# Hash attention with two MLP layers on one core: the products with the values of a pair of heads in one stretch of TensorE's queue, behind the projections for the next pair's hash bits

## The chip, the cores and the metric

The kernel runs on one core of one Trainium2 chip. The metric is the device time of one execution in microseconds (us). TensorE (PE in the profile) does all matrix products, VectorE (DVE) and ScalarE (ACT) read the products out of PSUM and do the elementwise work, GpSimd (POOL) does a little of it, and SyncE (SP) issues the DMAs.

## What is computed

The reference, cut to what matters here (scale is 1/8, B, H, S, D = 2, 8, 768, 64; n_bits is 6):

```python
q_bits = (np.einsum('bhsd,dk->bhsk', q, proj) > 0)      # the same for k
q_bucket = np.sum(q_bits * 2 ** np.arange(n_bits), axis=-1)
mask = q_bucket[:, :, :, None] == k_bucket[:, :, None, :]
scores = np.where(mask, scale * np.matmul(q, k.transpose(0, 1, 3, 2)), -1e9)
attn = np.exp(scores - np.max(scores, axis=-1, keepdims=True))
attn = attn / (np.sum(attn, axis=-1, keepdims=True) + 1e-09)
x = np.matmul(attn, v)                                  # heads joined: 1536 x 512
h = np.maximum(x @ w_in, 0.0)                           # first MLP, 512 -> 2048 -> 512
x = h * h @ w_out
h = x @ moe2_w_in                                       # second MLP, the same sizes
out = (np.maximum(h, 0.0) + alpha * np.minimum(h, 0.0)) @ moe2_w_out
```

A query attends only to the keys that have the same six sign bits. Everything is computed in float32, for the MLPs and the scores as sums of rounded high and low parts.

## The kernel before, in words

The 1536 tokens are four chunks of 384 (`T`). A chunk's attention is four pairs of heads; a pair lies with one head on partitions 0 to 63 and the other on 64 to 127. The attention of chunk 0 runs alone (`attention_first`). Then the first MLP of chunk c (`feed_forward`, lines 811 on) runs with the attention of chunk c + 1 woven into it (`attention_beside`): `attention_beside` returns a list of steps, and the object `following` calls the next of them at the slots of the MLP's loops. The last part, the second MLP (from line 1161 on), has no attention beside it. The change is in `attention_beside` alone, so in the twelve pairs of chunks 1 to 3.

For one such pair the work on TensorE is this. **The projections** (line 254 in `hash_bits`): the keys (`kr`, 768 columns, for an even chunk only, that is for the pairs of chunk 2, since chunk 3 uses the keys of chunk 2 again) and the queries (`qn`, 384 columns) are multiplied with `proj_sb`. The array is used as four strips of 32 columns, one for each quarter of the tokens, so that one product writes 32 partitions of the bank; VectorE makes bits of it (line 258). **The matches** (line 276): the bits with `code`, on the whole array. **The scores** (line 426): four products for each of the six blocks u of 128 queries (three blocks t for each head h), on the whole array; VectorE takes the maximum (`low`, line 434), ScalarE the exponential and its sum (`sm`, line 435). **The transposes** (line 451): six of `sm` per block, three to a bank `m`, copied to `pt` by ScalarE (456) or VectorE (458). **The products with the values** (line 472 in `blocks`): `vr`, six blocks of 128 keys, with `pt`. One head's product uses the left 64 columns of the array, the other's the right 64, twelve products in all, summed in one bank `o`, which ScalarE then copies to `u` (478). The profile has two instructions for each float32 product, so the twelve count as 24. **The reciprocal** (`recip`): a small transpose (486) of the sums, a copy `rrow` (488), a DMA to DRAM (498) and two back (`rb`, 501). `finish` multiplies `u` with `rb` and splits the result in `xh` and `xl` (517 to 519), which the next chunk's MLP reads.

The MLP's products beside it are lines 750 to 752 (hidden layer) and 791, 792, 795 (back to 512 columns), all on the whole array. While the two run side by side, the banks `m` are two, for the projections, the matches, the transposes, `o` and the reciprocal in turn; the scores have one pair of banks.

Each engine runs its own queue in the order in which the instructions stand there. The order is made when the kernel is built: steps in program order, and within that by priorities (`tc.high_priority`), so that an instruction of high priority is put ahead of others that are ready. Before the change, the three parts of the products with the values of a pair are three steps (`values(old, 0)`, then two more), woven between the MLP's products like every other step; the projections are made at the start of a pair's preparation (`first` for the keys, `q_split` for the queries). A pair's preparation runs during the pair ahead of it.

Of the kernel before, what the change touches and what calls it, by code (L numbers as in the profile page):

```python
# [9 lines left out]
BF16 = mybir.dt.bfloat16  # L10
U32 = mybir.dt.uint32
AX = mybir.AxisListType
AF = mybir.ActivationFunctionType
ALU = mybir.AluOpType
# [13 lines left out]
URGENT = 100  # L28
# [3 lines left out]
def kernel(  # L32
# [20 lines left out]
    nc = tc.nc  # L53
    B, H, D, S = qT.shape
    NB = N_BITS
    NT, DM = out.shape
    P = 128
# [154 lines left out]
    class Pair:  # L212
# [5 lines left out]
        def __init__(self, c, j):  # L218
            self.c, self.j = c, j
            self.b = c // 2  # L220
            self.first = c == 0 and j == 0
            self.awaited = c == 0 and j == NPAIR - 1
            self.p = {}
            self.pt = {}

        def pe(self, ins):

# [20 lines left out]
        def hash_bits(self, x, n):  # L248

            w = n // NG  # L250
            bits = p1.tile([P, S // NG], BF16, tag="bits", name="bits")[:, 0:w]
            ps = m_tile()
            for g in range(NG):
                self.pe(nc.tensor.matmul(
                    ps[g * GR:(g + 1) * GR, 0:w], proj_sb.rearrange("p h n -> p (h n)"), x[:, g * w:(g + 1) * w],
                    start=True, stop=True,
                ))
            self.next(nc.vector.tensor_scalar(bits, ps[:, 0:w], 0.0, None, ALU.is_gt))
            return bits

        def matches(self, bits, n):

# [33 lines left out]
                nc.sync.dma_start(out=f32(self.k[r, h]), in_=f32(kh[r]).unsqueeze(1).to_broadcast([D, 2, S]))  # L296

        def k_ids(self):
            y = self.matches(self.bits, S)
            ids = self.kr[:, 0].bitcast(F32R).rearrange("p (a n) -> p a n", n=T)  # L300
            for x, to in [(y[a], ids[:, a]) for a in range(2)] if self.c == 0 else [(y, ids)]:
                nc.vector.tensor_scalar(to, x, pop, -1.0, ALU.not_equal, ALU.mult)  # L302
            for h in range(2):
                r, o = self.rows(h)
                ins = nc.sync.dma_start(out=f32(self.k[o, h]), in_=self.kr[r])
            keyed[self.c, self.j] = ins

            tc.keep_in_program_order(load_values(self.b, self.j))
            self.vr = keys[self.b, self.j][-1]

        def q_split(self):
            self.new_q()
            self.bits = self.hash_bits(self.qn, T)
            if self.c == 0:
                for h in range(2):
                    self.q_halves(h)
                return
            self.q3 = state["q3"].tile([P, 3, T], F32R, tag="q3", name="q3")
            qh = self.q3[:, 1]
            nc.scalar.activation(qh, self.qn, AF.Copy, scale=scale)  # L320
            nc.vector.scalar_tensor_tensor(self.q3[:, 2], self.qn, scale, f32(qh), ALU.mult, ALU.subtract)
            for h in range(2):
                r, o = self.rows(h)
                nc.sync.dma_start(out=f32(self.q[r, h]), in_=f32(self.q3[r, 1:3]))
# [9 lines left out]
            ))  # L334

        def q_ids(self):
            y = self.matches(self.bits, T)
            if self.c == 0:
                self.q_yes(y)
                return  # L340
            nc.scalar.activation(self.q3[:, 0], y[:, 0, :], AF.Relu, bias=off, scale=FAR)
            for h in range(2):
                r, o = self.rows(h)
                nc.sync.dma_start(out=f32(self.q[o, h]), in_=f32(self.q3[r, 0:2]))
# [54 lines left out]
        def prepare(self):  # L399

            def ahead():
                c, j = divmod(self.c * NPAIR + self.j + 1, NPAIR)
                if c < NCH:
                    load_pair(c, j)

            def first():
                ahead()
                self.start()
                if self.c % 2 == 0:
                    self.k_bits()  # L410
                else:
                    self.q_split()

            if self.first:
                return [self.at_once, ahead]
            if self.c % 2:
                return [first, self.q_ids]
            return [first, self.k_split, self.k_ids, self.q_split, self.q_ids]
# [23 lines left out]
        def p_t(self, h, t, a):  # L442
            if t == 0 and a == 0:
                by = "third" if self.c == 0 and (2 * self.j + h) % 3 == 2 else "p2"
                self.pt[h] = state[by].tile([P, NTB, NKB, P], F32, tag="pt", name="pt")
            pp = self.p[h, t]
            ps = m_tile()
            n = NKB // 2
            for i in range(n):
                b = a * n + i  # L450
                self.pe(nc.tensor.transpose(ps[:, i * P:(i + 1) * P], pp[:, b * P:(b + 1) * P], ident))  # L451
            src = ps[:, 0:n * P].rearrange("p (b n) -> p b n", b=n)
            dst = self.pt[h][:, t, a * n:(a + 1) * n, :]
            with self.urgent():
                if EVICT[self.c][2 * t + a] == "a":
                    nc.scalar.activation(dst, src, AF.Copy)
                else:
                    nc.vector.tensor_copy(dst, src)  # L458

        def av(self, part):  # L460

            n = NKB // 3
            self.blocks(part * n, (part + 1) * n)

        def blocks(self, b0, b1, t0=0, t1=NTB):

# [104 lines left out]
    def attention_beside():  # L571
# [9 lines left out]
        def turn(pr, u):  # L581
            for a in range(2):
                steps.append(lambda a=a: pr.p_t(*divmod(u, NTB), a))

        def values(pr, part):
            steps.append(lambda: pr.av(part))

        def finish(pr):
            steps.append(pr.finish)
# [1 line left out]
                ends.append(len(steps))  # L591

        steps += [begin] + pairs[0].prepare()
        last = 2 * NTB - 1
        for n, pr in enumerate(pairs):
            old = pairs[n - 1] if n else None
            prep = pairs[n + 1].prepare() if n + 1 < len(pairs) else []
            for u in range(2 * NTB):
                steps.append(lambda pr=pr, u=u: pr.scores(*divmod(u, NTB)))
                if prep and u != 1:  # L600
                    steps.append(prep.pop(0))
                if u == 0 and old:
                    turn(old, last)
                    steps.append(old.recip)
                    values(old, 0)
                if u == 1 and old:
                    values(old, 1)
                    values(old, 2)
                if u:
                    turn(pr, u - 1)  # L610
                if u == 4 and prep:
                    steps.append(prep.pop(0))
                if u == (3 if old and old.j == NPAIR - 1 else last) and old:
                    finish(old)
            assert not prep
        turn(pr, last)
        steps.append(pr.recip)
        for part in range(3):
            values(pr, part)
        finish(pr)  # L620
        return steps, ends

# [635 lines left out]
```

## Time and profile before

| what | value |
|---|---|
| median of three runs | 787.2 us (785.86 to 789.8) |
| the profiled execution's own time | 787.25 us |
| its span from the first instruction to the last | 785.5 us |
| PE busy | 764.5 us, 97% of the span |
| DVE busy | 543.0 us, 69% |
| ACT busy | 509.8 us, 65% |
| POOL busy | 143.0 us, 18% |
| granted TensorE clock, mean | 0.997 of full speed |

The profile is of one execution. Its own time is 1.75 us longer than its span. An engine counts as busy while one of its instructions runs; waiting, branching and issuing DMAs don't count. Matmuls overlap each other, and their ends are modelled, so that the step from one start to the next is the better measure of what a product costs.

### The profile page before, as it was taken

Reading aid. Unit: us, or ns where it says so; the run is one execution under the profiler, and the core shown is the slowest. Engines: PE = TensorE matmul, PEld = TensorE weight load, DVE = VectorE, ACT = ScalarE, POOL = GpSimd, SP = SyncE. Lnnn points to the kernel's source line nnn. Section 1 sums busy time; section 2 is a strip of 40 time slices with the busy share of each in tenths; the row PEclk is TensorE's granted clock in tenths of the full one; section 3 lists DMA queues with packets and bytes.
Section 4 is the critical chain, followed back from the end, with each engine's and each line's share of the span. In section 5 each row is a group of like instructions: output and inputs, shape, how many; then the busy total and the mean of one; then the engine's idle time right before and its main releaser. Section 6 shows DMA issues by size and latency. Waiting matters only on the chain.

```text
span 785.5 us, 12375 instructions
## 1 busy us (share of the span) xinstructions
PE 764.5 (97%) x4354; PEld 633.0 (81%) x4354; DVE 543.0 (69%) x957; ACT 509.8 (65%) x990; POOL 143.0 (18%) x88
## 2 busy tenths in 40 slices
PE   6889999999999999999999999999999999999998
PEld 4556777877878777787787889999998889999886
DVE  7668789888778777997887856745665914666111
ACT  7769788777756646766675667856776534777331
POOL 1000000000000000000000001004657534657440
PEclk9999999999999999999999999999999999999999
DMA  5865888887878786887767685351311236321222
GB/s 164 216 191 188 250 279 266 273 231 224 227 237 255 213 237 219 304 256 268 243 214 238 202 281 203 113 163 60 129 41 55 67 109 224 130 75 51 58 67 93
DMA packets 56705, 143.65 MB, mean 183 GB/s; under 512 B 7402, under 2 KB 11652, under 8 KB 56644
## 3 DMA queue, kind: packets, MB, share of 16 engines
q1 hardware_dynamic: 56644, 142.87, 58.5%
q8 instruction: 34, 0.56, 0.3%
q14 instruction: 27, 0.22, 0.1%
HBM read 96.62 MB, written 25.47 MB: 155 GB/s over the span
## 4 chain that ended last, share of the span: by engine, by line
PE 62%; DVE 2%; DMA 2%; issue 0%; ACT 0%; SPq 0%; ACTq 0%
PE b L1081 6%; PE b L1080 6%; PE b L1086 5%; PE b L948 5%; PE b L947 5%; PE b L946 5%; PE m L472 3%; PE s L426 3%; PE h L750 3%; PE m L451 3%; PE h L752 2%; PE h L751 2%; PE acc L791 2%; PE acc L795 2%; PE acc L792 2%; PE acc L774 1%
## 5 line engine op out<-in xcount | busy, mean ns | idle before, releaser
L983 POOL TENSOR_TENSOR wp<-wraw,wp 128x1024 fp32r<-128x1024 f32 (+1 forms) x32 | 68.2, 2135 | 501.4 <-ACT wp L980 488.6
L712 ACT ACTIVATE wh<-wf 128x512 fp32r<-128x512 f32 x128 | 79.7, 629 | 55.2 <-PE h L751 24.4
L713 DVE TENSOR_TENSOR wl<-wf,wh 128x512 fp32r<-128x512 f32 x128 | 88.6, 699 | 32.9 <-ACT wh L712 32.6
L435 ACT ACTIVATE sm<-s,low 128x768 f32<-128x768 f32 x84 | 75.4, 898 | 35.7 <-DVE low L434 35.1
L434 DVE TENSOR_REDUCE low<-s 128x1 f32<-128x768 f32 x84 | 80.2, 955 | 14.6 <-PE s L426 13.1
L451 PE MATMUL m<-ident,sm 128*128 128x128 f32 x525 | 84.1, 276 | 4.7 <-DVE kr L302 1.6
L451 PEld LDWEIGHTS m<-ident,sm 128*128 128x128 f32 x525 | 64.1, 140 | 25.8 <-issue 2.7
L750 PE MATMUL h<-xh,wh 128*128 128x384 f32 x212 | 77.8, 367 | 1.2 <-ACT r L757 0.9
L426 PE MATMUL s<-k,q 128*128 128x384 f32 x336 | 77.7, 352 | 0.0
L1080 PE MATMUL b<-wp,gp 128*128 128x512 f32 x192 | 75.1, 391 | 0.0
L948 PE MATMUL b<-xph,wp 128*128 128x384 f32 x224 | 74.9, 334 | 0.0
L946 PE MATMUL b<-xph,wp 128*128 128x384 f32 x224 | 74.9, 334 | 0.0
L947 PE MATMUL b<-xpl,wp 128*128 128x384 f32 x224 | 74.9, 334 | 0.0
L1081 PE MATMUL b<-wp,gp 128*128 128x512 f32 x192 | 74.8, 390 | 0.0
L752 PE MATMUL h<-xh,wl 128*128 128x384 f32 x212 | 72.3, 341 | 0.0
L1070 POOL TENSOR_TENSOR gp<-g,gp 128x768 fp32r<-128x768 f32 x32 | 62.2, 1949 | 51.4 <-ACT gp L1067 50.7
L751 PE MATMUL h<-xl,wh 128*128 128x384 f32 x212 | 71.5, 337 | 0.0
L1064 DVE TENSOR_TENSOR wp<-wp 128x512 fp32r<-128x512 f32 x28 | 26.3, 950 | 61.7 <-ACT wp L1061 57.8
L426 PEld LDWEIGHTS s<-k,q 128*128 128x128 f32 x336 | 58.0, 190 | 10.5 <-ACT sm L435 3.7
L458 DVE COPY pt<-m 128x384 f32<-128x384 f32 x96 | 53.1, 553 | 18.5 <-PE m L451 17.9
L791 PE MATMUL acc<-wh,gh 128*128 128x512 f32 x144 | 64.6, 448 | 0.0
L792 PE MATMUL acc<-wl,gh 128*128 128x512 f32 x144 | 57.5, 399 | 0.0
(176 smaller groups left out, 1652.0 us busy)
## 6 DMA issues: line engine op xcount, KB each, us to landing
wf<-w SPq DMA_DIRECT2D x96, 256.0 KB, 3.1
wbits<-in_w_in_dram SPq DMA_DIRECT2D x32, 512.0 KB, 4.3
wbits<-in_w_out_dram SPq DMA_DIRECT2D x32, 512.0 KB, 4.7
wraw<-ws SPq DMA_DIRECT2D x16, 896.0 KB, 6.7
q<-q SPq DMA_DIRECT2D x48, 192.0 KB, 3.9
w<-wf SPq DMA_DIRECT2D x32, 256.0 KB, 4.2
wp<-w SPq DMA_DIRECT2D x32, 256.0 KB, 2.6
k<-kh SPq DMA_DIRECT2D x14, 384.0 KB, 6.1
```

What stands on the lines that cost most here:

```text
L426: self.pe(nc.tensor.matmul(ps[:, a, 0:HALF], self.q[:, h, i, qs], self.k[:, h, i, ks], start=i == 0, stop=i == 1))
L451: self.pe(nc.tensor.transpose(ps[:, i * P:(i + 1) * P], pp[:, b * P:(b + 1) * P], ident))
L713: nc.vector.tensor_tensor(lo, w, f32(hi), ALU.subtract)
L750: nc.tensor.matmul(hp, wih[:, ks], xh[:, kk, :], start=first, stop=False)
L751: nc.tensor.matmul(hp, wih[:, ks], xl[:, kk, :], start=False, stop=False)
L752: nc.tensor.matmul(hp, wil[:, ks], xh[:, kk, :], start=False, stop=last)
L791: nc.tensor.matmul(acc[t], gh[:, blocks[t]], woh, start=first, stop=False)
L946: nc.tensor.matmul(ps, w[0][:, ms], gh, start=first, stop=False, skip_group_check=True)
L947: nc.tensor.matmul(ps, w[0][:, ms], gl, start=False, stop=False, skip_group_check=True)
L948: nc.tensor.matmul(ps, w[1][:, ms], gh, start=False, stop=last, skip_group_check=True)
L1080: nc.tensor.matmul(a, g[:, 0, b], w[:, 0], start=f == 0, stop=False)
L1081: nc.tensor.matmul(a, g[:, 0, b], w[:, 1], start=False, stop=False)
```

## The change

A pair's twelve products with the values are issued in one step, `row`, at the second block of scores (u = 1) of the pair that follows. In front of them stand the projections of the pair to come: `all_bits` makes those of the keys (chunk 2) and of the queries in one bank, with one copy to `bits` by VectorE. Both have a priority of 200 over the rest, so nothing of the MLP is put in between. The first projection also waits for the two last copies to `pt` of the pair whose values follow (`behind`, the list `turned`). The reciprocal's step comes behind the row instead of ahead of the values. In the lines below, 222 to 484 are methods of `Pair`, the last hunks are in `attention_beside`.

```diff
--- before.py
+++ after.py
@@ -222,6 +222,7 @@
             self.awaited = c == 0 and j == NPAIR - 1
             self.p = {}
             self.pt = {}
+            self.turned = []
 
         def pe(self, ins):
 
@@ -248,7 +249,7 @@
         def hash_bits(self, x, n):
 
             w = n // NG
-            bits = p1.tile([P, S // NG], BF16, tag="bits", name="bits")[:, 0:w]
+            bits = p1.tile([P, (S + T) // NG], BF16, tag="bits", name="bits")[:, 0:w]
             ps = m_tile()
             for g in range(NG):
                 self.pe(nc.tensor.matmul(
@@ -257,6 +258,31 @@
                 ))
             self.next(nc.vector.tensor_scalar(bits, ps[:, 0:w], 0.0, None, ALU.is_gt))
             return bits
+
+        def all_bits(self, behind):
+
+            x = ([] if self.c % 2 else [self.kr[:, 1]]) + [self.qn]
+            ends = [0]
+            for a in x:
+                ends.append(ends[-1] + a.shape[-1] // NG)
+            ps = m_tile()
+            for a, n0, n1 in zip(x, ends, ends[1:]):
+                w = n1 - n0
+                for g in range(NG):
+                    ins = nc.tensor.matmul(
+                        ps[g * GR:(g + 1) * GR, n0:n1], proj_sb.rearrange("p h n -> p (h n)"),
+                        a[:, g * w:(g + 1) * w], start=True, stop=True,
+                    )
+                    for e in behind:
+                        tc.add_manual_dep(
+                            ins.ins, e.ins.name,
+                            mybir.DependencyInfo(mybir.DependencyClass.Sync, mybir.DependencyReason.DATA),
+                            reason="in a row with the products with the values",
+                        )
+                    behind = []
+            bits = p1.tile([P, (S + T) // NG], BF16, tag="bits", name="bits")
+            nc.vector.tensor_scalar(bits[:, 0:ends[-1]], ps[:, 0:ends[-1]], 0.0, None, ALU.is_gt)
+            self.k_code, self.q_code = bits[:, 0:ends[-2]], bits[:, ends[-2]:ends[-1]]
 
         def matches(self, bits, n):
 
@@ -296,7 +322,7 @@
                 nc.sync.dma_start(out=f32(self.k[r, h]), in_=f32(kh[r]).unsqueeze(1).to_broadcast([D, 2, S]))
 
         def k_ids(self):
-            y = self.matches(self.bits, S)
+            y = self.matches(self.k_code if self.c else self.bits, S)
             ids = self.kr[:, 0].bitcast(F32R).rearrange("p (a n) -> p a n", n=T)
             for x, to in [(y[a], ids[:, a]) for a in range(2)] if self.c == 0 else [(y, ids)]:
                 nc.vector.tensor_scalar(to, x, pop, -1.0, ALU.not_equal, ALU.mult)
@@ -310,8 +336,8 @@
 
         def q_split(self):
             self.new_q()
-            self.bits = self.hash_bits(self.qn, T)
             if self.c == 0:
+                self.bits = self.hash_bits(self.qn, T)
                 for h in range(2):
                     self.q_halves(h)
                 return
@@ -334,7 +360,7 @@
             ))
 
         def q_ids(self):
-            y = self.matches(self.bits, T)
+            y = self.matches(self.q_code if self.c else self.bits, T)
             if self.c == 0:
                 self.q_yes(y)
                 return
@@ -406,10 +432,10 @@
             def first():
                 ahead()
                 self.start()
-                if self.c % 2 == 0:
+                if self.c % 2:
+                    self.q_split()
+                elif not self.c:
                     self.k_bits()
-                else:
-                    self.q_split()
 
             if self.first:
                 return [self.at_once, ahead]
@@ -453,14 +479,10 @@
             dst = self.pt[h][:, t, a * n:(a + 1) * n, :]
             with self.urgent():
                 if EVICT[self.c][2 * t + a] == "a":
-                    nc.scalar.activation(dst, src, AF.Copy)
+                    ins = nc.scalar.activation(dst, src, AF.Copy)
                 else:
-                    nc.vector.tensor_copy(dst, src)
-
-        def av(self, part):
-
-            n = NKB // 3
-            self.blocks(part * n, (part + 1) * n)
+                    ins = nc.vector.tensor_copy(dst, src)
+            self.turned = self.turned[-1:] + [ins]
 
         def blocks(self, b0, b1, t0=0, t1=NTB):
 
@@ -582,8 +604,13 @@
             for a in range(2):
                 steps.append(lambda a=a: pr.p_t(*divmod(u, NTB), a))
 
-        def values(pr, part):
-            steps.append(lambda: pr.av(part))
+        def row(old, new):
+
+            with tc.high_priority(offset=2 * URGENT):
+                if new:
+                    new.all_bits(old.turned if old else [])
+                if old:
+                    old.blocks(0, NKB)
 
         def finish(pr):
             steps.append(pr.finish)
@@ -591,6 +618,7 @@
                 ends.append(len(steps))
 
         steps += [begin] + pairs[0].prepare()
+        steps.insert(-1, lambda: pairs[0].all_bits([]))
         last = 2 * NTB - 1
         for n, pr in enumerate(pairs):
             old = pairs[n - 1] if n else None
@@ -601,11 +629,11 @@
                     steps.append(prep.pop(0))
                 if u == 0 and old:
                     turn(old, last)
-                    steps.append(old.recip)
-                    values(old, 0)
-                if u == 1 and old:
-                    values(old, 1)
-                    values(old, 2)
+                if u == 1:
+                    new = pairs[n + 1] if n + 1 < len(pairs) else None
+                    steps.append(lambda old=old, new=new: row(old, new))
+                    if old:
+                        steps.append(old.recip)
                 if u:
                     turn(pr, u - 1)
                 if u == 4 and prep:
@@ -614,9 +642,8 @@
                     finish(old)
             assert not prep
         turn(pr, last)
+        steps.append(lambda: row(pr, None))
         steps.append(pr.recip)
-        for part in range(3):
-            values(pr, part)
         finish(pr)
         return steps, ends
 
```

How this moves TensorE's queue, at three places. In these listings, taken from the built programs, a row is an instruction or several equal ones (x4), with its line in its own kernel, what it writes and what it reads; lines 254, 426, 451, 472, 486, 750 to 752, 791, 792, 795 of before are 272, 452, 477, 494, 508, 777 to 779, 818, 819, 822 of the changed kernel.

Before, on TensorE, during the scores of chunk 2's last pair (the values are those of the pair ahead of it):

```order
L472 MATMUL m<-pt,vr 64x384 x3
L426 MATMUL s<-k,q 128x384 x4
L472 MATMUL m<-pt,vr 64x384
L750 MATMUL h<-xh,wh_3605 128x384
L751 MATMUL h<-xl,wh_3605 128x384
L752 MATMUL h<-xh,wl_3606 128x384
L750 MATMUL h<-xh,wh_3605 128x384
L751 MATMUL h<-xl,wh_3605 128x384
L752 MATMUL h<-xh,wl_3606 128x384
L472 MATMUL m<-pt,vr 64x384 x3
L426 MATMUL s<-k,q 128x384 x4
L472 MATMUL m<-pt,vr 64x384
```

The same values in the changed kernel, with the transposes (line 477) ahead of them:

```order
L819 MATMUL acc_2959<-wl_3503,gh 128x512
L818 MATMUL acc_2960<-wh_3502,gh 128x512
L819 MATMUL acc_2960<-wl_3503,gh 128x512
L477 MATMUL m<-ident,sm 128x128 x6
L818 MATMUL acc_2961<-wh_3502,gh 128x512
L819 MATMUL acc_2961<-wl_3503,gh 128x512
L822 MATMUL acc_2959<-wh_3502,gl 128x512
L272 MATMUL m<-qn,proj_sb 32x96 x4
L494 MATMUL m<-pt,vr 64x384 x12
L452 MATMUL s<-k,q 128x384 x4
L822 MATMUL acc_2960<-wh_3502,gl 128x512
L822 MATMUL acc_2961<-wh_3502,gl 128x512
```

Eight products of the values stood in four pieces (and four more just ahead of these rows); now all twelve follow each other behind the projections of the queries, three MLP products behind the transposes whose copies they wait for.

Before, on TensorE, the projections of the keys of a pair of chunk 2, alone among MLP products:

```order
L751 MATMUL h<-xl,wh_3120 128x384
L752 MATMUL h<-xh,wl_3121 128x384
L254 MATMUL m<-kr,proj_sb 32x192 x4
L750 MATMUL h<-xh,wh_3120 128x384
L751 MATMUL h<-xl,wh_3120 128x384
```

Now:

```order
L819 MATMUL acc_2961<-wl_3110,gh 128x512
L822 MATMUL acc_2959<-wh_3109,gl 128x512
L272 MATMUL m<-kr,proj_sb 32x192 x4
L272 MATMUL m<-qn,proj_sb 32x96 x4
L494 MATMUL m<-pt,vr 64x384 x12
L452 MATMUL s<-k,q 128x384 x4
```

The projections of the keys and of the queries have moved together, and the row's products with the values of another pair behind them.

Before, on TensorE, the last pair of all, with its reciprocal's transpose (line 486) first:

```order
L486 MATMUL m<-ident,rin 6x128
L791 MATMUL acc_4537<-wh_5447,gh 128x512
L792 MATMUL acc_4537<-wl_5448,gh 128x512
L795 MATMUL acc_4535<-wh_5447,gl 128x512
L795 MATMUL acc_4536<-wh_5447,gl 128x512
L795 MATMUL acc_4537<-wh_5447,gl 128x512
L472 MATMUL m<-pt,vr 64x384 x4
```

Now the last rows of this pair:

```order
L494 MATMUL m<-pt,vr 64x384 x5
L778 MATMUL h<-xl,wh_5516 128x384
L779 MATMUL h<-xh,wl_5517 128x384
L777 MATMUL h<-xh,wh_5516 128x384
L778 MATMUL h<-xl,wh_5516 128x384
L779 MATMUL h<-xh,wl_5517 128x384
L777 MATMUL h<-xh,wh_5516 128x384
L778 MATMUL h<-xl,wh_5516 128x384
L779 MATMUL h<-xh,wl_5517 128x384
L508 MATMUL m<-ident,rin 6x128
```

The last pair's values stand in two pieces, seven products and five, and its reciprocal, which stood ahead of all three of its pieces, now stands behind them.

Over the whole of chunks 1 to 3 the program before has 33 unbroken pieces of products with the values, and 17 of projections apart from the first two; in four places a piece of the values ends after an odd number of products. The changed program has 13 pieces of values (eleven of twelve products, then seven and five). Ten of the eleven have projections directly ahead of them, four of these of keys and queries and six of queries alone, and there are no other projections but the first two.

## Rows read from the trace of the kernel before

**Rows 1.** Busy us (instructions) of PE, PEld, DVE, ACT, POOL, 85 to 460 us; clock, DMA.

```profile
85.00:460.00 375.00, 372.33 (x2185) 289.21 (x2183) 310.60 (x580) 254.65 (x516) 0.00 (x0) 1.00 0.78 242
```

**Rows 2.** Timeline of PE around pieces of eight and of sixteen instructions (start, us).

```profile
450.92 0.34 PE L752 MATMUL h<-xh,wl 128*128 128x384 f32 x1
451.19 1.51 PE L472 MATMUL m<-pt,vr 128*64 128x384 f32 x8
...
452.92 0.34 PE L751 MATMUL h<-xl,wh 128*128 128x384 f32 x1
453.09 0.34 PE L752 MATMUL h<-xh,wl 128*128 128x384 f32 x1
...
259.11 2.80 PE L472 MATMUL m<-pt,vr 128*64 128x384 f32 x16
...
262.12 0.33 PE L751 MATMUL h<-xl,wh 128*128 128x384 f32 x1
```

**Rows 3.** Timeline of PE around a piece of one product (two instructions).

```profile
354.55 0.86 PE L472 MATMUL m<-pt,vr 128*64 128x384 f32 x2
...
355.63 0.34 PE L751 MATMUL h<-xl,wh 128*128 128x384 f32 x1
```

**Rows 4.** Timeline of PE around projections of queries, and of keys.

```profile
131.63 0.37 PE L254 MATMUL m<-qn,proj_sb 128*32 128x96 f32 x8
...
132.21 0.34 PE L751 MATMUL h<-xl,wh 128*128 128x384 f32 x1
...
250.37 0.53 PE L254 MATMUL m<-kr,proj_sb 128*32 128x192 f32 x8
...
251.12 0.34 PE L751 MATMUL h<-xl,wh 128*128 128x384 f32 x1
```

**Rows 5.** Timeline of PE in chunk 0: projections with values directly behind them.

```profile
32.95 0.37 PE L254 MATMUL x<-qn,proj_sb 128*32 128x96 f32 x8
33.25 1.51 PE L472 MATMUL h<-pt,vr 128*64 128x384 f32 x8
```

**Rows 6.** Lines 472 and 254: instructions, ns min/median/max, first and last start us.

```profile
L472 PE MATMUL m<-pt,vr x288: 485/487/538, 113.0 to 454.9; 128*64 128x384 f32 x144
...
L254 PE MATMUL m<-qn,proj_sb x80: 245/258/271, 108.5 to 381.7; 128*32 128x96 f32 x80
```

**Rows 7.** Timeline: last transposes of two pairs, and the copies to pt.

```profile
446.34 0.49 PE L451 MATMUL m<-ident,sm 128*128 128x128 f32 x3
...
447.03 0.47 ACT L456 ACTIVATE pt<-m 128x384 f32<-128x384 f32 x1
...
447.14 0.27 PE L486 MATMUL m<-ident,rin 128*6 128x128 f32 x1
...
252.02 0.38 PE L451 MATMUL m<-ident,sm 128*128 128x128 f32 x2
...
254.15 0.55 DVE L458 COPY pt<-m 128x384 f32<-128x384 f32 x1
...
254.41 0.90 ACT L435 ACTIVATE sm<-s,low 128x768 f32<-128x768 f32 x1
```

**Rows 8.** Timeline of DVE, SP and PE at the end of the last pair; then the DMAs' landing.

```profile
448.14 0.27 DVE L488 COPY rrow<-m 6x128 f32<-6x128 f32 x1
...
450.96 1.09 SPq L501 DMA_DIRECT2D rb<-rin  x2
...
465.31 0.33 PE L750 MATMUL m<-xh,wh 128*128 128x384 f32 x1
...
rb<-rin SPq DMA_DIRECT2D x30, 96.0 KB, 3.3
```

**Rows 9.** Timeline of DVE and SP at another pair's reciprocal.

```profile
287.10 0.28 DVE L488 COPY rrow<-m 6x128 f32<-6x128 f32 x1 [0.40 <-PE m L486]
...
295.49 0.48 SPq L498 DMA_DIRECT2D rin<-rrow  x1
```

**Rows 10.** Line 478 (the copy u): count, ns min/median/max, first and last start us.

```profile
L478 ACT ACTIVATE u<-m x12: 469/491/497, 118.1 to 455.4; 128x384 f32<-128x384 f32 x12
```

## The prediction

> **What bounds the kernel now.** I read first the busy times of the stretch in which the change lies, 85 to 460 us [rows 1]. TensorE (the first pair of numbers) is busy 372.3 of 375.0 us at a granted clock of 1.00, VectorE 310.6, ScalarE 254.7. So TensorE never waits for long there: 2.7 us in all. The reader is to see that a microsecond taken from TensorE's queue here can be a microsecond of the kernel, as long as nothing else makes it wait: VectorE has 64 us of room, ScalarE 120. A busy TensorE is not one that streams columns all the time, though, so I went on to its timeline and read it by the steps from one start to the next.
>
> An MLP product follows its neighbour by 0.17 us (452.92 to 453.09 [rows 2]). Around a piece of products with the values the steps are longer. In the piece of eight instructions, from the start of the product ahead of it (450.92) to the start of the second behind it (452.92) there are 2.00 us; less two ordinary steps, 1.66 us are the piece's own. From a piece's start to that second product eight instructions take 1.73 us (451.19 to 452.92) and sixteen 3.01 (259.11 to 262.12) [rows 2]. So eight more cost 1.28 us, 0.16 each, and of the 1.66 some 0.38 belong to no product: they are paid once for a piece, on its way in and out. The starts are rounded to 0.01, and I take **0.36 us for a piece**. The eight with 128 columns ahead and behind is the commonest case.
>
> **What the change takes away and adds.** (1) Pieces. Of the 288 instructions of line 472 [rows 6] there are 33 pieces before and 13 now. The projections (80 instructions for queries, first and last at 108.5 and 381.7 [rows 6], and those for the keys) make 17 pieces before, which now lie in ten of the 13. That is 50 against 13: 37 pieces fewer, 37 x 0.36 = 13.3 us.
>
> (2) Odd cuts. Two products on the two halves of the columns run at the same time, so a product that is cut off from its partner costs as much as a pair. The piece of one product shows it: from its start to the second product behind it there are 1.08 us [rows 3]. By the numbers above a piece of two instructions of a pair would have 1.73 - 1.28 + 0.32 = 0.77, so the lone product costs 0.31 more; its partner on the other side of the cut does the same, 0.62 for a cut. Four such cuts before, one now (seven and five, at the last pair): 3 x 0.62 = 1.9 us.
>
> (3) Change of width. In ten of the new rows 32 columns change to 64 in the middle. Alone, the projections of the queries have 0.58 us from their start to the second product behind them [rows 4], of which 1.73 - 1.28 = 0.45 belong to any piece, so the work itself is 0.13. In chunk 0 the same projections stand directly ahead of values, and there the values start 0.30 us behind them [rows 5]. The change of width costs 0.17, ten times 1.7 us. The keys' projections keep their own work (0.75 - 0.45 = 0.30 [rows 4]) in either order. The bounds are nothing and a whole piece's price of 0.36, so 0 to 3.6 us; I take the row, since it is the very sequence. The Trainium skill, TensorEngine Tiling (Array Packing), section Key Properties, says that changing the tiling mode, and not just the tile, drains TensorE; by it the step from 32 to 64 columns is a drain like any other, and if that were as dear as a whole piece the sum would come out 1.9 us later. The trace shows half of that at this very step.
>
> The sum on TensorE is 13.3 + 1.9 - 1.7 = 13.5 us less.
>
> (4) The wait at a row's head. The first projection now waits for the two last copies to `pt` of the pair whose values follow. Everything behind it on TensorE waits too: the values, the next scores, and all MLP products. What is late is the copy. In an ordinary case the last three transposes start at 446.34 and their copy ends at 447.50 (447.03 + 0.47), 1.16 us later; in the worst one the first of its transposes started at 252.02 and the copy on VectorE ended at 254.70, 2.68 us later [rows 7]. As cover the changed program has between three and seven MLP products behind the transposes: with two of them there are 0.80 us from 446.34 to 447.14 [rows 7], so about 1.0 with three. Ordinary copies are thus late by 0.1 to 0.2 in the tightest rows and not at all in the others, and the worst by 1.7. Bounds for eleven rows are nothing and 18 us. I take 0.15 us a row, 1.6 us, since most copies look like the first one. The waits that the stretch has now (2.7 us) I leave as they are.
>
> (5) The bits. One copy on VectorE in place of two, for four pairs; the keys' low parts (line 293) now wait for the row, and behind them on VectorE stand the weights' low parts. VectorE's 64 us cover that; without cover it would be the row's delay again, and it is in the range of (4). The matches of a pair find their bits earlier than before.
>
> (6) The reciprocal comes behind the values. Within the chunks `finish` is two blocks or more away. At the end it is not: the next chunk's MLP needs `xh` of the last pair. In the trace `rrow` starts at 448.14, its DMAs back are issued from 450.96 on and land 3.3 us later, near 455 [rows 8], so 8 us from the small transpose at 447.14 [rows 7]; with the product by `rb` and the rounding, one after the other on two engines and each about as long as the copy `u` (0.49 [rows 10]), 9 us. Before, the MLP asked for the result only at 465.31 [rows 8]. In the changed order 27 products of 512 and 22 of 384 columns stand between; at 0.17 us for 384, and so 0.23 for 512 (an estimate by columns), that is 9.9 us. That leaves 0.9 us; I charge 0.5.
>
> **The sum.** The profiled execution took 787.25 us, beside a median of 787.2, and its span lies 1.75 us inside; nothing outside the span changes. 787.25 - 13.5 + 1.6 + 0.5 = 775.85, so **775.9 us**.
>
> **Rivals.** *The rows' heads give half of it or all of it back.* If each of eleven rows waits 0.6 us, the time is 787.25 - 13.5 + 6.6 + 0.5 = 780.9; at 1.2 us a row it is 787.5 and nothing is left. For it speak the 2.68 us of [rows 7]; against it that most copies end 1.2 us behind their transposes and TensorE hardly waits anywhere now [rows 1]. The Trainium skill, TensorE: Matmul & The Clock Gate, section The mechanism (What overlaps and what doesn't), has matmuls start in strict order, with no reordering; by it the engine can't fill such a wait with the MLP's products behind it.
>
> *The row's end makes it slower.* A row holds both banks `m`: the bits' and `o`. The next transposes need a bank, so they wait for the copy `u` (0.49 us [rows 10]) on ScalarE. Four scores (0.7 us) and the small transpose cover it, if ScalarE does it at once. If an exponential of the scores behind the row went first, `u` would be late by those four scores, their maximum and the exponential (0.90 [rows 7]), 2.3 us or more with the maximum about as long as the exponential, so 28 us over twelve pairs and about 802 us. It decides from (13.5 + 3.9) / 12 = 1.4 us a pair on. In ScalarE's queue of the changed program `u` stands ahead of that exponential in all twelve pairs, which speaks against it.
>
> *The end of the attention is held by a DMA.* SyncE issues in order, and a pair's first DMA left 8.4 us behind its data once (287.10 to 295.49 [rows 9]). If that befalls the last pair, 7 us go: 783.
>
> *The change does nothing*, because the pieces don't stay whole: the listings show that they do. Or because another engine bounds the stretch: rows 1 speak against it.
>
> **How the numbers follow.** The forecast (773 to 779) has a chance of 0.56; half given back 0.12; all of it given back, 783.3 to 791, 0.14; slower by the row's end 0.08; the held end 0.05; less than 772, if neither heads nor width cost anything, 0.05. The measurement can tell about 0.5% from no change, so below 783.3 is faster and above 791.1 slower: faster 0.56 + 0.12 + 0.05 + 0.05 = 0.78, same 0.14, slower 0.08. The range from 772 to 787 leaves out 0.05 below and the dearest cases above, about 0.15.
>
> **What would show it.** In the profile after: 13 pieces of values; each with 0.30 us between the queries' projections and the values; 24 instructions in a piece at 0.16 us each; TensorE's busy time about 11 to 13 us less; idle time in front of the projections under 0.3 us a row, ended by a copy to `pt`. Wrong would be: a row that begins more than 0.5 us behind the product ahead of it as a rule, transposes behind the rows that wait for `u`, or a gap of several us ahead of the last chunk's first hidden product.

## The result, and the profile after

The changed kernel takes 779.7 us (median of six, 777.9 to 782.2) against 787.5 of the kernel before (six, 785.9 to 789.8): a ratio of 0.9897, 95% interval 0.9871 to 0.9922. So it is 7.7 us faster, where 11.4 were forecast (787.25 to 775.85). The profiled execution was the slowest of the six, 782.16 us with a span of 780.1; what it shows at its dearest place need not be paid in full by the usual execution.

First the busy times of the stretch of [rows 1] in the changed kernel, and those of the stretch behind it (columns as there):

```profile
85.00:460.00 375.00, 369.95 (x2235) 300.59 (x2228) 312.95 (x583) 257.51 (x526) 0.00 (x0) 1.00 0.81 250
455.00:480.00 25.00, 22.39 (x125) 21.75 (x124) 11.93 (x16) 15.82 (x30) 4.51 (x2) 0.93 0.73 246
```

The reader is to see two things: more instructions fit into the same 375 us (2235 on TensorE against 2185), but TensorE is busy 2.4 us less of them, so it waits more (over the whole span it is busy 753.8 us, where it was 764.5); and from 455 to 480 us, where it was busy all of the 25.00 us before, 2.6 us are idle and the granted clock is 0.93.

The rows themselves are as ordered. Timeline of TensorE around one with the projections of the queries, and then the values' line by itself (count, ns min/median/max, first and last start), which answer to [rows 2, 5, 6]:

```profile
137.37 0.33 PE L777 MATMUL h<-xh,wh 128*128 128x384 f32 x1
137.63 0.37 PE L272 MATMUL m<-qn,proj_sb 128*32 128x96 f32 x8
137.94 4.09 PE L494 MATMUL m<-pt,vr 128*64 128x384 f32 x24
141.96 0.97 PE L452 MATMUL s<-k,q 128*128 128x384 f32 x4
142.77 0.33 PE L778 MATMUL h<-xl,wh 128*128 128x384 f32 x1
```

```profile
L494 PE MATMUL m<-pt,vr x288: 486/486/537, 113.1 to 443.7; 128*64 128x384 f32 x144
```

The values start 0.31 us behind the projections (0.30 forecast). From the product ahead (137.37) to the product behind the scores (142.77) there are 5.40 us; the five whole-array products in it take 0.174 each, so the row's own price is 4.53. Read in this way for every piece, with the step behind it, all pieces cost 69.5 us before and 56.1 now. The difference of 13.4 us is what TensorE saves on them. It depends a little on the steps that are taken as ordinary ones: with 0.174 us for 384 columns and 0.23 for 512 the two sums are 70.2 and 56.6, so a few tenths of such sums are the method's.

What TensorE waited for from 85 to 475 us (total us, times, longest), where it was 2.7 us before, none of it at the end:

```profile
PE s L452 <- ACT sm L461: 2.9, 5, 0.9
PE m L911 <- DMA wf<-w: 2.6, 1, 2.6
PE h L777 <- ACT r L784: 1.2, 1, 1.2
PE m L302 <- ACT pt L482: 0.7, 2, 0.5
```

Line 272, the projections at a row's head, is not among them: the heads hardly wait (0.11 us of idle time once, 0.3 us in all by the steps). Nothing on TensorE waits there for `u` (line 500). Scores (452) wait for the exponential of the scores ahead, since they have one pair of banks. One such wait, on ScalarE and then TensorE:

```profile
337.15 0.63 ACT L739 ACTIVATE wh<-wf 128x512 fp32r<-128x512 f32 x1 [1.20 <-DMA wf<-w]
337.69 0.88 ACT L461 ACTIVATE sm<-s,low 128x768 f32<-128x768 f32 x1
...
338.72 0.96 PE L452 MATMUL s<-k,q 128*128 128x384 f32 x4 [0.87 <-ACT sm L461]
```

The exponential stood behind the rounding of a weight whose load was late. The MLP's products behind the scores (339.51 on) read no result of an exponential, but stood still too, as the Trainium skill, TensorE: Matmul & The Clock Gate, section The mechanism (What overlaps and what doesn't), has it: matmuls start in strict order.

The largest wait is new: line 911 transposes `yb`, the first MLP's result of chunk 0, which is loaded back at the end of the attention, into memory that was the attention's. SyncE's timeline there, VectorE's and TensorE's:

```profile
446.33 0.29 SPq L520 DMA_DIRECT2D rin<-rrow  x1
446.72 2.35 SPq L757 DMA_DIRECT2D wf<-w  x3
450.86 1.09 SPq L523 DMA_DIRECT2D rb<-rin  x2
451.99 1.48 SPq L757 DMA_DIRECT2D wf<-w  x2
453.81 0.32 SPq L996 DMA_DIRECT2D wraw<-ws  x1
455.87 0.32 SPq L887 DMA_DIRECT2D y<-y  x1
457.04 0.32 SPq L904 DMA_DIRECT2D yb<-y  x1
...
445.92 0.28 DVE L510 COPY rrow<-m 6x128 f32<-6x128 f32 x1
...
455.78 0.56 DVE L541 TENSOR_TENSOR xl<-u,xh 128x384 fp32r<-128x384 f32 x1
...
463.79 0.34 PE L801 MATMUL s<-gh,wl 128*128 128x384 f32 x1
466.73 1.09 PE L911 MATMUL m<-ident,yb 128*128 128x128 f32 x4 [2.61 <-DMA wf<-w]
```

And the view of the tile `yb`, how long its load took, and two of SyncE's waits from 440 to 475 us:

```profile
DMA to landing us min/median/max: 9.2/9.2/9.2
...
SPq L996 <- PE m L508: 1.8, 1, 1.8
SPq L523 <- DMA rin<-rrow: 1.8, 1, 1.8
```

The bracket names another load (`wf`), but the transposes read only `ident` and `yb`: `yb`'s load was issued at 457.04 and landed 9.2 us later, 0.5 us ahead of their start.

The last reciprocal holds SyncE's queue twice, 1.8 us each time: a first load of `wraw` (line 996, weights of the second MLP) waits for the reciprocal's transpose (line 508) and leaves at 445.92, and `rb` waits for `rin` until 450.86 ([rows 8] before). Behind them a second load of `wraw`, 0.92 MB, a store of `y` and the load of `yb` come close together, and `yb` lands after 9.2 us. Its transposes stand where they stood before, 56 listed rows behind the first product of the last MLP; before the load was issued at 466.0 and they ran at 473.5, 7.5 us later, without a wait. Now they would run 6.9 us behind it. By two-microsecond stretches TensorE's clock (the figure ahead of the last two) also falls to half behind this wait:

```profile
464.00:466.00 2.00, 0.12 (x1) 0.00 (x0) 2.00 (x2) 0.29 (x1) 1.01 (x1) 1.00 0.27 105
466.00:468.00 2.00, 1.27 (x6) 1.30 (x7) 0.03 (x1) 0.14 (x1) 0.00 (x0) 0.56 0.78 236
468.00:470.00 2.00, 2.00 (x9) 2.00 (x8) 0.20 (x1) 1.32 (x3) 0.00 (x0) 0.59 0.75 307
470.00:472.00 2.00, 2.00 (x13) 2.00 (x12) 1.09 (x2) 0.69 (x2) 0.00 (x0) 1.00 0.20 38
```

### The profile page after: what moved, and what is told of

The parts are those of the page before. It is cut to its first block, busy times and chain, and to the rows that moved or that the text cites. A ratio compares the mean times of both kernels' runs of the same rounds, so it can differ in the third digit from the quotient of the medians.

```text
span 780.1 us, 12405 instructions
## 1 busy us (share of the span) xinstructions
PE 753.8 (97%) x4354; PEld 636.7 (82%) x4354; DVE 536.3 (69%) x953; ACT 508.0 (65%) x990; POOL 143.9 (18%) x88
## 4 chain that ended last, share of the span: by engine, by line
PE 86%; DMA 5%; ACT 4%; DVE 3%; issue 1%; SPq 0%; ACTq 0%; DVEq 0%
PE s L452 7%; PE m L477 6%; PE b L1107 6%; PE b L1108 6%; PE m L494 5%; PE b L1113 5%; PE b L975 5%; PE b L973 5%; PE b L974 5%; PE h L777 4%; PE h L778 4%; PE h L779 4%; PE acc L818 4%; PE acc L819 4%; PE acc L822 4%; DMA wf<-w 3%
## 5 line engine op out<-in xcount | busy, mean ns | idle before, releaser
L477 PE MATMUL m<-ident,sm 128*128 128x128 f32 x525 | 81.8, 274 | 4.9 <-DVE kr L328 1.9
L777 PE MATMUL h<-xh,wh 128*128 128x384 f32 x212 | 75.9, 358 | 1.4 <-ACT r L784 1.2
L1091 DVE TENSOR_TENSOR wp<-wp 128x512 fp32r<-128x512 f32 x28 | 24.0, 864 | 65.4 <-ACT wp L1088 65.4
L818 PE MATMUL acc<-wh,gh 128*128 128x512 f32 x144 | 62.8, 436 | 0.0
```

The source lines that it names most:

```text
L777: nc.tensor.matmul(hp, wih[:, ks], xh[:, kk, :], start=first, stop=False)
L818: nc.tensor.matmul(acc[t], gh[:, blocks[t]], woh, start=first, stop=False)
```

## The experiments

The edits are cut to the lines that matter. The theory: TensorE's saving is the price of the pieces, as the sum had it, and what is missing was given back at the end (`yb`) and in front of scores. Rivals: the rows' heads wait; odd cuts and widths cost otherwise; the late reciprocal is harmless. Times are medians, ratios are to the kernel before on the same chip (787.2 to 788.5 us). "Own price" is the sum over all pieces read as above, waits inside them included unless said.

**Values alone in a row.** In `row` only the values are left; the projections go back to `hash_bits`:

```diff
             with tc.high_priority(offset=2 * URGENT):
-                if new:
-                    new.all_bits(old.turned if old else [])
                 if old:
                     old.blocks(0, NKB)
```

> Only the values of a pair stand in one row; the projections stay alone, where they were before the change. 31 pieces instead of 51 (the first two projections counted in). Theory (every piece costs 0.36 us, an odd cut 0.62): 20 fewer pieces 7.2 us, one odd cut fewer 0.6, no change of width: 7.8 us less on TensorE, of which some 2 to 4 come back as waits at the end of the attention and in front of the scores: 781.5 to 784. Rival (the price belongs to the projections, or to the rows' ends): less than 2 us of gain, 786 or more.

781.7 us, ratio 0.9917 (0.9886 to 0.9947). Own price 63.2 us, of which 1.5 are waits inside two pieces; without them, and without the 0.5 of such waits before, 7.3 us less than before (7.8 expected). A wait for `yb` of 1.3 us is there too. So the values alone bring more than half of the saving (6.5 us between the two medians).

**Projections alone together.** The values are in three parts as before, the projections by `all_bits([])` at u = 1:

```diff
-                    old.blocks(0, NKB)
+        def values(pr, part):
+            n = NKB // 3
+            steps.append(lambda: pr.blocks(part * n, (part + 1) * n))
```

> Only the projections of keys and queries stand together, at the changed place; the values are in three parts as before, and the scheduler puts projections into the middle of their pieces. 35 pieces instead of 51, but 18 changes of width inside pieces, and about 11 odd cuts of the values where there were 4. Theory: 16 pieces less 5.8 us, 7 odd cuts more 4.3, 18 changes of width 3.1: plus 1.6 us on TensorE, 787 to 790. Rival (neither odd cuts nor changes of width cost what was taken for them): 5.8 less, about 782.

791.1 us, ratio 1.0031 (1.0015 to 1.0047): slower, with fewer pieces, and 1.1 us above the expected range. Own price 71.2 us, 1.7 more than before (2.2 if the 0.5 of waits in pieces before are left out). What it looks like, on TensorE:

```profile
113.34 1.50 PE L494 MATMUL m<-pt,vr 128*64 128x384 f32 x6
114.78 0.37 PE L272 MATMUL m<-qn,proj_sb 128*32 128x96 f32 x8
115.08 0.86 PE L494 MATMUL m<-pt,vr 128*64 128x384 f32 x2
115.87 0.96 PE L452 MATMUL s<-k,q 128*128 128x384 f32 x4
116.76 2.80 PE L494 MATMUL m<-pt,vr 128*64 128x384 f32 x16
```

Two instructions of the values take 0.79 us from their start to the next scores (115.08 to 115.87), because their partner on the other half of the columns stands ahead of the projections. The three prices together foretold a loss where pieces alone would have foretold 5.8 us of gain.

**Rows cut in the middle.**

```diff
-                    old.blocks(0, NKB)
+                    old.blocks(0, NKB // 2)
+        def rest(old):
+            old.blocks(NKB // 2, NKB)
```

> The changed kernel with each row cut in the middle: the second six products are a step of their own without the priority, so that MLP products, scores and transposes come between. 29 pieces (with the first projections) instead of 14, and four odd cuts instead of one. Theory: 15 x 0.36 = 5.4 and 3 x 0.62 = 1.9, so 7.3 us more on TensorE, 63.4 us for all pieces, and 5 to 7.5 us more than the changed kernel beside it. Rival (what the row saves lies in the projections' place and the order, not in the number of pieces): within 2 us of the changed kernel.

784.7 us, ratio 0.9956 (0.9944 to 0.9969): 5.4 more than the changed kernel beside it (779.3). Own price 63.2 us (63.4 expected), 7.1 more than in the changed kernel (7.8 with the other ordinary steps given above, of which 0.9 are waits inside two pieces). Here the end of the attention lies later, the second `wraw` load leaves behind `yb`'s (467.78 and 464.38), `yb` lands after 5.7 us, and nothing waits for it; so the time differs by less than the own price.

**Heads without the wait.**

```diff
-                    new.all_bits(old.turned if old else [])
+                    new.all_bits([])
```

> The changed kernel without the wait of the projections for the copies to pt. The scheduler then puts projections ahead of the values by themselves in eight pairs more: 22 pieces instead of 14. Theory: 8 pieces more 2.9 us, 8 changes of width fewer 1.4, waits at the heads hardly any (0.2): plus 1.3 us against the changed kernel, about 781. Rival (the wait at the rows' heads is what gives back the missing 4 to 5 us): 775 to 777.

780.0 us, ratio 0.9890 (0.9866 to 0.9914), like the changed kernel. Own price 58.9 us, 2.8 more than there, 1 us of it a wait inside one row. The wait at the heads costs nothing that matters; its use is to keep projections and values together.

**Transposes of `yb` later.**

```diff
-        [(0.0, 0), (0.01, 1), (0.13, 1), (0.9, 2 * (1 + NTB) + 7)],
+        [(0.0, 0), (0.01, 1), (0.2, 1), (0.9, 2 * (1 + NTB) + 7)],
```

> The changed kernel, with the first transposes of yb 27 places later in TensorE's queue. Theory (at the end of the attention 2.6 us and the clock's drop behind them are lost to these transposes, which wait for a load): the gap and the half clock are gone from the profile, and the median falls by what the usual execution pays of it, 1 to 3.5 us: 776 to 778.5. Rival (the load is late because something else is, which then waits in its place): 779 to 780.5.

778.2 us, ratio 0.9855 (0.9830 to 0.9880). No gap and a clock of 1.00 from 455 to 480 us; the profiled execution took 775.9.

**The last reciprocal ahead of its row.**

```diff
         turn(pr, last)
-        steps.append(lambda: row(pr, None))
         steps.append(pr.recip)
+        steps.append(lambda: row(pr, None))
```

> The changed kernel with the reciprocal of the very last pair ahead of its row again, as before the change. Its row is then whole, twelve products: one piece and one odd cut fewer, 1.0 us. Theory (the wait for yb comes from its load, which can't start before the first hidden group of the last MLP has run and then takes 9 us): that group no longer waits for the last pair, so the load starts some 0.6 us sooner, but the gap ahead of the transposes of yb stays, 1.5 to 2.5 us; in all 1 to 2 us less than the changed kernel. Rival (the late reciprocal is what opens the gap): gap gone, 3.5 to 5 us less.

775.9 us, ratio 0.9845 (0.9825 to 0.9866), 3.5 less than the changed kernel beside it. SyncE and TensorE at the end:

```profile
440.86 1.09 SPq L523 DMA_DIRECT2D rb<-rin  x2
442.05 0.54 SPq L757 DMA_DIRECT2D wf<-w  x1
442.68 0.37 SPq L996 DMA_DIRECT2D wraw<-ws  x1
443.79 3.54 SPq L757 DMA_DIRECT2D wf<-w  x4
447.37 0.43 SPq L996 DMA_DIRECT2D wraw<-ws  x1
452.01 0.32 SPq L887 DMA_DIRECT2D y<-y  x1
453.32 0.32 SPq L904 DMA_DIRECT2D yb<-y  x1
...
460.58 0.34 PE L801 MATMUL s<-gh,wl 128*128 128x384 f32 x1
460.76 0.60 PE L911 MATMUL m<-ident,yb 128*128 128x128 f32 x4
```

My theory had the gap stay; the rival had it go, and it went. The second `rb` leaves 9.7 us ahead of the hidden layer's first product (451.0) instead of 2.7 us, and both `wraw` loads leave some 6 us or more ahead of `yb`'s. That opens the question whether the lateness itself or the crowd of loads makes the gap. The last row is whole here, 1.0 us less as expected (4.17 against 2.87 + 2.28).

**`wraw` behind `yb`, reciprocal late.** The two loads are ordered behind the load of `yb` in SyncE's queue, nothing else:

```diff
+    with tc.issue_after(state["yb", 0].ins):
-    w_load(0)
-    w_load(1)
+        w_load(0)
+        w_load(1)
```

> The changed kernel, last reciprocal behind its row, but with the two loads of 0.92 MB each for the second MLP (wraw) put behind the load of yb in SyncE's queue. Theory (the late reciprocal's rb holds back the loads behind it in SyncE's queue, which then run into the load of yb): with 0.92 MB less just ahead of it, yb lands some 3 us sooner, in 6 to 7 us instead of 9.2 to 9.4, the gap ahead of its transposes shrinks from 2.7 to under 0.7, and the time by 1.5 to 3 us, to 776.5 to 778. Rival (the load starts late because the first hidden group is late, and takes its 9 us whatever runs beside it): a gap of over 2 us, and 779 to 780.

777.7 us, ratio 0.9869 (0.9840 to 0.9898). SyncE and TensorE:

```profile
448.72 1.09 SPq L523 DMA_DIRECT2D rb<-rin  x2
449.92 2.71 SPq L757 DMA_DIRECT2D wf<-w  x3
455.04 0.32 SPq L887 DMA_DIRECT2D y<-y  x1
455.93 0.32 SPq L904 DMA_DIRECT2D yb<-y  x1
...
463.19 0.34 PE L801 MATMUL s<-gh,wl 128*128 128x384 f32 x1
463.36 0.60 PE L911 MATMUL m<-ident,yb 128*128 128x128 f32 x4
```

The reciprocal still stands behind its row, and the gap is gone. `rb` leaves 4.9 us ahead of the hidden layer's first product (453.6) here, where no `wraw` load waits in front of it, and 3.2 us ahead in the changed kernel; but what has changed for `yb` is the load ahead of it. It lands within the 7.4 us up to its transposes, where it took 9.2 with `wraw` ahead, and 5.7 in the kernel with the cut rows, which has no `wraw` just ahead either. So the crowd does it: a big load that the waits for the reciprocal in SyncE's queue have pushed close ahead of `yb`'s. What this is worth in time is not clear of the noise: the interval of the ratio overlaps with those of the changed kernel.

**Both mends.** Reciprocal ahead and transposes later together:

> Both mends together: the last reciprocal ahead of its row and the first transposes of yb 27 places later. Theory: 1.0 us for the whole row, up to 0.6 for the hidden group, and what the kernel with the later transposes alone gave: 3 to 4.5 us less than the changed kernel, 775 to 777. Rival (the two mends take away the same wait): no better than the later transposes alone, 777 to 778.5.

777.5 us, ratio 0.9866 (0.9844 to 0.9887). No better than either alone, as the rival had it: they take away the same wait.

**The changed kernel again.**

> The changed kernel itself, as the measure for the three beside it on this chip: 778 to 782; the gap ahead of the transposes of yb between 1.5 and 3 us, and the half clock behind it not in every execution.

779.3 us (777.7 to 781.4), ratio 0.9893 (0.9874 to 0.9912), a gap of 2.7 us ahead of line 911. Waits for the exponential were 4.5 us in this profile, 2.9 in the first.

**Loads of bits one step sooner.** On top of the last reciprocal ahead:

```diff
+    loads, uses = steps[0::2], steps[1::2]
+    steps = loads[:1] + [s for pair in zip(loads[1:], uses) for s in pair] + uses[-1:]
```

> The kernel with the last reciprocal ahead of its row, and in addition the loads of the second MLP's weight bits (wbits) one step of the conversion sooner, so that ScalarE waits less for them. Theory (the scores wait for the exponential because it stands in ScalarE's queue behind conversions and roundings whose loads are late): ScalarE's waits for wbits fall from 10.2 us to under 4, TensorE's waits for the exponential from 2.4 to about 1, and the time by 1 to 1.5 us, to 774.5. Rival (the exponentials are late by ScalarE's own work, or another load takes the place): within 0.8 us of 775.9 or above it.

778.6 us, ratio 0.9881 (0.9850 to 0.9912): no better, a miss. ScalarE waited 5.5 us for the bits instead of 10.2, but 7.0 for `w`'s stores (`w<-we`) instead of 3.1, and TensorE longer for the exponential:

```profile
PE s L452 <- ACT sm L461: 4.5, 5, 2.2
```

**All three mends.**

> Last reciprocal ahead of its row, the wbits loads one step sooner and the wraw loads behind yb, all three. If each mend takes away a wait of its own: 773 to 775, no gap ahead of the transposes of yb. If the last two change nothing that the first has not changed: 775.5 to 777.

778.8 us, ratio 0.9889 (0.9859 to 0.9920). No gap for `yb`, but above both expectations. Of the kernels with whole rows and without the gap, the two with the sooner bits have the highest ratios; that the bits give back what the others bring is likely and not shown, since the intervals overlap.

**Half of the conversion left out.** On top of the last reciprocal ahead:

```diff
-            steps += [lambda u=u: load_bits(u), lambda u=u: ahead(u)]
+            steps += [lambda: None, lambda u=u: w_d.update({u: w_d[0, u[1], 1]})]
```

> The kernel with the last reciprocal ahead of its row, without the conversion of the second MLP's output weights (16 times a load of bits, ScalarE 0.67 us, VectorE twice and a store, between 190 and 440 us); the second MLP reads the first one's output weights instead, so this part of the result is left out. Theory (scores wait for an exponential that stands behind conversions whose data are late): of TensorE's waits for the exponential behind 190 us, 2.2 us in the kernel it is made from, 1 us or less is left, and the time is 1 to 2.5 us under that kernel, 773.5 to 775. Rival (the waits come from the order of scores and exponentials alone): waits and time as in that kernel, 775.5 to 777.

777.4 us, ratio 0.9858 (0.9841 to 0.9875). TensorE's waits from 190 to 455 us:

```profile
PE s L452 <- ACT sm L461: 1.3, 3, 0.7
PE s L452 <- DMA q<-q: 1.1, 2, 0.9
PE m L302 <- DVE pt L484: 1.0, 1, 1.0
PE m L477 <- DVE rrow L510: 0.6, 1, 0.6
PE m L272 <- ACT pt L482: 0.4, 1, 0.4
```

Waits for the exponential fell from 2.1 to 1.3 us and others came in their place. Late conversions make single waits, but taking work away doesn't make the kernel faster: the cause of these small waits as a whole is not found.

## Why the prediction was right in direction and 4 us short

The measured 779.7 us lies in the range of 772 to 787, but just above the 773 to 779 that had the highest chance, in the band of the rival that the rows' heads give half of it back (0.12). The heads gave back next to nothing. So the saving came about as forecast, and what reduced it was something else, which the prediction had put at 0.5 us or at nothing; that the total is also that rival's is chance.

*Steps 1 to 3, the pieces*: right. 13.5 us forecast, 13.4 measured as own price, and the three kernels that change the count of pieces, odd cuts and widths came out at -7.3, +1.7 and +7.1 us of own price for -7.8, +1.6 and +7.3. TensorE's busy time fell by 10.7 us, a little under the 11 to 13 forecast. A row with queries costs 4.52 and one without projections 4.22: the change of width and the work are 0.30, as taken. The Trainium skill, TensorEngine Tiling (Array Packing), section Key Properties, says that a change of the tiling mode drains TensorE. The trace agrees, and better than the prediction read it: a piece has two such changes, in and out, for 0.36 us together, and the change of width is one, for about 0.17. The prediction's upper bound for it, a whole piece's 0.36, set one change against two.

*Step 4, the heads*: 1.6 us charged, 0.1 to 0.3 measured; freeing them changed nothing. Wrong was the sentence beside it, "The waits that the stretch has now (2.7 us) I leave as they are": outside the pieces the steps from 84 to 462 us, less what each kind of product takes undisturbed, add up to 11.6 us where they were 8.1, 3.5 more. In four other profiles of kernels with whole rows (the later transposes, the early reciprocal, the changed kernel again, `wraw` behind `yb`) it is 1.0, 1.3, 3.7 and 2.5 more (1.6, 1.8, 3.8 and 2.6 with the other ordinary steps given above, so about half a microsecond of each is the method's). What makes these waits, beyond single cases like the one at 338.72, stays open. A step tells more here than the idle time in brackets: a product shows as busy for 0.33 us where the step is 0.17, which hides the first 0.16 of a wait.

*Step 5*: nothing, as forecast; VectorE has its room still. The row's end cost nothing either, `u` was in time.

*Step 6, the reciprocal behind the values*: the step that was mis-sized. It looked at who reads the result (the hidden layer's product, which indeed hardly waits) and charged 0.5. It did not look at what stands in SyncE's queue behind the DMAs that wait for the reciprocal. The gap there is 2.6 us, 2.8 by steps, and the half clock behind it costs another 1.4 in the profiled execution (from 466.73 to the eighth product behind the transposes 3.04 us, the same in the kernel with the early reciprocal 1.66). Taking it away gave 3.5 us between two medians on one chip, 1.0 of them from the whole last row. The rival of the held DMA named the right queue and the wrong victim: the gap came not ahead of the first hidden product, where the prediction would have looked for it, but ahead of `yb`'s transposes.

The account of the profiled execution: 787.25 - 13.4 + 3.5 + 2.8 + 1.4 = 781.55, against 782.16; 0.6 us have no name. It is the slowest of the six; the median of 779.7 has no profile of its own. Without the gap, by its ratio and the 787.5 us, the kernel with the early last reciprocal takes 775.3 us and the one that only moves `wraw` 777.2, beside the forecast of 775.9. The lowest ratio found is the former's, 0.9845; its interval lies below that of the changed kernel beside it, but overlaps with those of the other kernels with whole rows and without the gap.

## What to carry to other kernels

Price a tiled piece among whole-array products by three figures, entry and exit, halves that lost their partner, and changes of width; here the sums held to about half a microsecond over five orders of the same work. When a step moves, list not only who waits for its result but what stands behind its DMAs on their queue, and whether the next bulk transfers then meet. And don't carry the waits of the kernel before over unchanged: here, with 13 us taken from the busiest engine, a load and some exponentials that had been in time were late.

## What was not expected of the hardware

Where TensorE was idle for 2.61 us, the granted clock fell to 0.56 and 0.59 in the next two stretches above, that is for the most part to the lower of its two levels (1.2 GHz), but in the changed kernel's second profile, at an idle 2.73 us in the same place, it stayed at 1.00. The load of `yb`, 0.79 MB, took 9.2 us with 0.92 MB and a store ahead of it, less than 7.5 without the former in the kernel with `wraw` behind `yb`, and 5.7 in the kernel with the cut rows.
